# First block's second norm emitted earlier, its rows put into the query weights' tile, with closer weight slices

## The chip, the cores and the metric

The kernel runs on one core of one Trainium2 chip. The core has five engines that take their instructions from five queues, each in its own order: TensorE (PE: matrix products, with weight loads as a row of their own, PEld), VectorE (DVE), ScalarE (ACT), GpSimd (POOL) and SyncE (SP, which here only issues DMAs). An instruction waits at the head of its queue until the semaphores that it needs are set, and whatever stands behind it on that engine waits too. The metric is device microseconds of one execution: 1638.99 us is the median of three runs of the kernel before (1636.83 to 1641.09).

## The reference

One transformer block on 2048 rows of 512, with modulation by a vector c:

```python
mod = (_silu(c) @ w_mod).reshape(c.shape[0], 6, 1, -1)
sa, ca, ga, sb, cb, gb = (mod[:, 0], mod[:, 1], ..., mod[:, 5])
h = _layernorm(x, axis=-1) * (1 + ca) + sa
x = x + ga * _A_ref(h, A_wq, A_wk, A_wv, A_wo)      # 32 heads of 16, one k and one v for all heads
h = _layernorm(x, axis=-1) * (1 + cb) + sb
x = x + gb * _B_ref(h, B_w_gate, B_w_up, B_w_down)  # (h W_gate * h W_up) W_down, 1792 columns
```

The attention is an exact softmax: scores over 2048 keys, their maximum taken out, exponential, product with v, division by the sum, then the product with wo.

## The kernel before, in words

**Units and turns.** The 2048 rows are eight blocks (`sb`, 0 to 7) of 256 query rows. A block has four groups of 8 heads, so there are 32 units `u` (unit 5 is block 1, second group of heads). A unit runs through 16 key tiles of 128 keys, one per *turn*; `attend(u, kt)` writes out two turns. Time in the program is counted in *steps*, two per turn and 32 per unit, so step 176 is unit 5, turn 8. In every turn stand four score products for the exponentials (`sc`, L680 and L682, with their four ACT exponentials, L688), four score products that only serve the maximum of the next unit (`mx`, L610, each followed by a DVE maximum over 512 keys, L614), and eight float32 products of the exponentials with v (`pv`, L722), which need the exponentials of the turn before or of this turn's first half.

**Side work.** All other large products run as *side* groups (class `Group`, L519) in PSUM banks of their own: the q projection (`q_proj`, 16 groups), the wo product (`wo_work`), and per block 14 gate/up groups and two down groups of the FFN (`ffn_work`). Between the score products, which use 48 or 51 of the 128 rows of the PE array, stand *halves* of side products on 64 rows, so that two such products run beside each other. A turn is written in one of three styles: FEW has four side halves, MANY has eight, and NO_SIDE has none, because no side group may start. What may start is decided by `open_gate`: the FFN groups of block `sb` wait for `h2done`, that is for the block's second norm. Side work that has found no place by the last unit is done after it, in the *tail*, with whole products on 128 rows.

**The second norm of a block.** When a block's wo group ends, `wo_work`'s `fin` adds the residual on DVE (L808), takes statistics on DVE (`spread` L815, `aggr` L818) and then 1/sqrt on POOL: eight short instructions, `rv` to `nb` (L220 to L225, L821, L822). `nrm` then makes the normed rows `n2`; for block 0 that is one ACT instruction per 128 rows (L829), which reads what POOL has made. For block 0 (and 7) `ln2_work` transposes `n2` on PE in two *turns* of four transposes (L880), ACT puts scale and shift in (`hf`, L888), and POOL splits the result into a high and a low float16 half (L893, L894), into the tile `h2T`. Blocks 1 to 6 make their `h2` with DMA transposes. For block 0 `nrm` was put 7 and 12 ticks (a tick is half a turn) behind the end of the second wo group, and the two transposing turns were taken only when all q groups had ended (`all(q.ended() for q in qs)`), because `h2T` was a new tile on the place of the q weights `wq`.

**Weights.** `late_weights` loads 4 slices of wo, 32 of gate and up (128 x 448) and 14 of down. A slice is loaded by SP (L1022) into one of six places of the staging tile `kwb` and split on POOL two list items later in three instructions (L1164 or L1158, L1165, L1166). Items are spaced by `SPLIT_GAP` steps. The squares of the down rows for their norms are ACT instructions between them (L1076).

**q groups.** They read column block `ch` of `wq` (128 columns each). The last three are block 3's second to fourth, and two of these run behind the wo groups of block 0.

**PSUM.** Eight banks; `pv` and the running side group hold one each, and `sc` and `mx` products go round the rest in the order in which banks were used.

Of the kernel before, what the change touches and what calls it, by code (L numbers as in the profile page):

```python
# [34 lines left out]
SLOTS = (0, 1, 2, 3, 12, 13)  # L35
SUM_GAP = 4.0
SUM_LAG = 3
SPLIT_GAP = 2.5
LAST_GAP = 2.5
LATE_Q = 3  # L40
NORM_AT = (2, 9, 12, 16)
NBANK = 8
QPRE = 24
Q_LAG = 8
TR_WAIT = 11
TR_LAG = 4
H2_LAG = 2
NHF = 12
# [20 lines left out]
def adaln_mqa_glu_kernel(ctx: ExitStack, tc: tile.TileContext, x_in, wq_in, wk_in, wv_in, wo_in,  # L69
# [627 lines left out]
    def p_places(both):  # L697
        n = 9 * D
        for i in range(2):
            t = both[:, i * n:(i + 1) * n]  # L700
            p_sets.append((t[:, D:].bitcast(F32).rearrange("p (j t) -> p j t", j=4),
                           t[:, :8 * D].rearrange("p (j h t) -> p j h t", j=4, h=2)))
        for i, k in enumerate(kts16):
            nc.gpsimd.tensor_scalar(v16[:, 0, i], vst[:, k, :], 1.0, 0.0, op0=OP.mult, op1=OP.add)
            nc.gpsimd.tensor_tensor(v16[:, 1, i], vst[:, k, :], v16[:, 0, i], op=OP.subtract)

    def pv(v):
        u, kt = divmod(v, KT)
# [83 lines left out]
    def wo_work(sb):  # L792
        on_pool = 2 <= sb < NS - 2
        by_dma = 0 < sb < NS - 1

        def op(t):
            def f(i):
                ch, term = divmod(i, 3)
                ol, wl = TERMS[term]
                return [(och[sb, ch][:, ol, t * 128:(t + 1) * 128], wo[:, wl, ch, :])]  # L800
            return f

        def fin(t):
            row = 2 * sb + t

            def f(p):
                x1 = x1s[row]
                nc.vector.scalar_tensor_tensor(x1, p, sca[:, 7:8], x1, op0=OP.mult, op1=OP.add)  # L808
                s2 = work.tile([128, 1, 2], F32, name="st2", bufs=5)
                bs = work.tile([128, 6], F32, name="bs", bufs=4)  # L810
                nb = work.tile([128, 2], F32, name="nb", bufs=4)
                yt = {}

                def spread():
                    nc.vector.bn_stats(bs, x1)  # L815

                def aggr():
                    nc.vector.bn_aggr(s2[:, 0, :], bs)  # L818
                    yt["y"] = rstd_of(s2, 1)
                    if not on_pool:  # L820
                        nc.gpsimd.tensor_tensor(nb[:, 0:1], s2[:, 0, 0:1], yt["y"], op=OP.mult)  # L821
                        nc.gpsimd.tensor_scalar(nb[:, 1:2], nb[:, 0:1], -1.0, 0.0, op0=OP.mult, op1=OP.add)  # L822

                def nrm():
                    n2 = work.tile([128, D], F32, name="n2", tag="n2", bufs=2)
                    if on_pool:
                        nc.gpsimd.tensor_scalar(n2, x1, s2[:, 0, 0:1], yt["y"], op0=OP.subtract, op1=OP.mult)
                    else:
                        nc.scalar.activation(n2, x1, AF.Identity, bias=nb[:, 1:2], scale=yt["y"])  # L829
                    n2s[row] = n2  # L830
                    if not by_dma:
                        return
                    nc.gpsimd.tensor_tensor(n2, n2, cbb, op=OP.mult)
                    nc.gpsimd.tensor_tensor(n2, n2, sbb, op=OP.add)
                    n16 = work.tile([128, 2, D], F16, name="n16", tag="gf", bufs=4)
                    nc.gpsimd.tensor_scalar(n16[:, 0, :], n2, 1.0, 0.0, op0=OP.mult, op1=OP.add)
                    nc.gpsimd.tensor_tensor(n16[:, 1, :], n2, n16[:, 0, :], op=OP.subtract)
                    after(TR_LAG + (3 if sb < 2 else 0), lambda: ln2_turn(sb, t, n16))

                after(3, spread)  # L840
                after(4, aggr)
                n2f[row] = nrm
                if t == 1:
                    late = 3 if sb < 2 else 0
                    for j in range(2):
                        after((4, 9)[j] + late, n2f[2 * sb + j])
                    if sb == 0:
                        after(TR_WAIT + late, lambda: turns.extend(ln2_work(sb)))
            return f

        return [Group(3 * KC, op(t), fin(t), lambda t=t: load_x(2 * sb + t)) for t in range(2)]
# [12 lines left out]
    def ln2_work(sb):  # L864
        st = {}

        def tr(i):
            def f():
                if not h2s:
                    h2T = big.tile([128, 2, 2, KC, ST], F16, name="h2T", tag="wq")  # L870
                    both = big.tile([128, 2 * KC * S], F16, name="glu", tag="big")
                    n = 2 * FT * ST
                    glus.append(both[:, :n].rearrange("p (h f t) -> p h f t", h=2, f=FT))
                    p_places(both[:, n:])
                    h2s.update({s: h2T[:, s % 2] for s in range(NS)})
                st["p"] = ps_hold("mx")
                for k in range(2):
                    for t in range(2):
                        c = k * ST + t * 128
                        nc.tensor.transpose(st["p"][:, c:c + 128],  # L880
                                            n2s[2 * sb + t][:, (2 * i + k) * 128:(2 * i + k + 1) * 128], ident)
            return f

        def ev(i):
            def f():
                hf = work.tile([128, 2, ST], F32, name="hf", tag="g", bufs=2)
                for k in range(2):
                    nc.scalar.activation(hf[:, k, :], st["p"][:, k * ST:(k + 1) * ST], AF.Identity,  # L888
                                         bias=hsc[:, 2 * i + k, 0:1], scale=hsc[:, 2 * i + k, 1:2])
                ps_give(st["p"])  # L890
                eng = nc.vector if sb == NS - 1 else nc.gpsimd
                h = h2s[sb][:, :, 2 * i:2 * i + 2, :]
                eng.tensor_scalar(h[:, 0], hf, 1.0, 0.0, op0=OP.mult, op1=OP.add)  # L893
                eng.tensor_tensor(h[:, 1], hf, h[:, 0], op=OP.subtract)  # L894
# [14 lines left out]
    def ffn_work(sb):  # L909

        def glu():
            return glus[0]

        def op(f):
# [390 lines left out]
    def attend(u, kt):  # L1305
# [10 lines left out]
        def end_turn(kt):  # L1316
# [8 lines left out]
            v = pv_place(u * KT + kt - 1) if u + kt else None  # L1325
            if v is not None:
                pv(v)
            if not late_max() and turns and all(q.ended() for q in qs):
                _, f, post = turns.popleft()
                f()  # L1330
                posts.append(post)
# [36 lines left out]
    def hooks(u, i):  # L1368
        step = u * NSTEP + i
        if later_h and i % 2 and i > 4:  # L1370
            b1, k = later_h.popleft()
            h_halves(b1, (k,))
        side_step(step)
        since = i - out_at[0]
        if u > 0 and i >= 3 and since in NORM_AT:
# [95 lines left out]
```

## Time and profile before

| | |
|---|---|
| median of three runs | 1638.99 us (1636.83 to 1641.09) |
| the profiled execution's own time | 1637.85 us |
| its span, first to last instruction | 1635.6 us |
| mean granted TensorE clock | 0.997 |
| DVE maxima L614 | 2016 instructions, 1273.0 us busy |
| ACT exponentials L688 | 1824 + 224 instructions, 982.5 + 123.8 us busy |
| PE whole gate products L519 on 128 rows | 292 instructions, 64.0 us busy |
| PE half gate products L519 on 64 rows | 2104 instructions, 476.5 us busy |

Rows of a timeline read: start in us, duration in us, engine, line, operation, written tile <- read tiles, shape, how many merged, and in brackets the engine's idle time before it with what ended it. Rows that group instructions read: count, busy us, mean ns of one, and the idle time before them. PE rows overlap, since products are pipelined; the distance between starts is what a product costs.

### The profile page before, as it was taken

How to read it: one execution, taken by the hardware profiler on the slowest of the kernel's cores; microseconds unless marked ns; L12 is line 12 of the kernel's file. 1: busy time of each engine (PE TensorE's matmuls, PEld its weight loads, DVE VectorE, ACT ScalarE, POOL GpSimd, SP SyncE). 2: the span in 40 equal slices, each digit the busy share in tenths (PEclk: the TensorE clock that was granted, in tenths of full speed). 3: DMA queues.
4: the chain of work that ended last, by engine and by line, in shares of the span. 5: the costliest groups of instructions: out<-in, count | busy, mean ns of one | idle time of the engine just before them, and what ended most of it. 6: DMA issues, size and time to landing. Idle time of an engine off the chain costs nothing.

```text
span 1635.6 us, 41004 instructions
## 1 busy us (share of the span) xinstructions
PE 1617.4 (99%) x15853; PEld 746.9 (46%) x15853; DVE 1401.3 (86%) x2433; ACT 1220.8 (75%) x2421; POOL 955.7 (58%) x1316
## 2 busy tenths in 40 slices
PE   8999999999999999999999999999999999999999
PEld 4333333355533555335543455434545345444766
DVE  8999999899999999999999999999999999980211
ACT  6688878888777888778877788777878778878300
POOL 6857537875755566646656466653657556565422
PEclk9999999999999999999999999999999999999999
DMA  7213314243221001100011001100001001100100
GB/s 257 99 56 97 94 63 122 89 128 93 65 63 35 14 20 29 36 32 20 13 32 36 26 14 33 32 26 26 20 25 33 24 18 33 32 15 22 34 14 14
DMA packets 78994, 79.13 MB, mean 48 GB/s; under 512 B 30408, under 2 KB 59340, under 8 KB 78800
## 3 DMA queue, kind: packets, MB, share of 16 engines
q1 hardware_dynamic: 77744, 76.46, 14.9%
q8 instruction: 124, 2.03, 0.5%
q14 instruction: 70, 0.57, 0.1%
q10 hardware_dynamic: 1056, 0.07, 0.0%
HBM read 56.04 MB, written 17.05 MB: 45 GB/s over the span
## 4 chain that ended last, share of the span: by engine, by line
PE 93%; ACT 2%; POOL 2%; DVE 2%; issue 1%; DMA 0%; SPq 0%; ACTq 0%; POOLq 0%; DVEq 0%
PE side L519 42%; PE pv L722 29%; PE mx L610 8%; PE sc L682 8%; PE sc L680 3%; ACT P L688 1%; DVE mpart L614 1%; PE part L290 0%; DMA wmA<-in_w_mod_dram 0%; PE mxt L638 0%; PE pk L298 0%; PE sc L610 0%; POOL wg L1166 0%; POOL kwb L1164 0%; POOL q L556 0%
## 5 line engine op out<-in xcount | busy, mean ns | idle before, releaser
L614 DVE TENSOR_REDUCE mpart<-mx 128x1 f32<-128x512 f32 x2016 | 1273.0, 684 | 81.7 <-PE mx L610 73.9
L688 ACT ACTIVATE P<-sc 128x512 f32<-128x512 f32 x1824 | 982.5, 599 | 219.6 <-PE sc L682 177.4
L610 PE MATMUL mx<-kst,sst 48*128 48x512 f16 x2032 | 629.0, 377 | 2.1 <-ACT P L688 0.9
L682 PE MATMUL sc<-sst,kst 51*128 51x512 f16 x1792 | 597.7, 379 | 0.8 <-ACT P L688 0.3
L519 PE MATMUL side<-h2T,wg 64*128 64x256 f16 (+1 forms) x2396 | 540.5, 271 | 0.6 <-POOL h2T L893 0.3
L519 PE MATMUL side<-h2T,wu 64*128 64x256 f16 (+1 forms) x2396 | 538.2, 270 | 0.0
L722 PE MATMUL pv<-P,vst 128*32 128x512 f32 x3648 | 485.7, 605 | 0.7
L519 PEld LDWEIGHTS <-wg 64*128 64x128 f16 (+1 forms) x2396 | 226.0, 94 | 220.1 <-ACT P L688 160.4
L519 PE MATMUL side<-wd,glu 64*128 64x512 f16 (+1 forms) x1172 | 271.7, 377 | 0.4 <-ACT tok L685 0.2
L695 POOL TENSOR_TENSOR glu<-glu 128x512 f16<-128x512 f32 x224 | 259.4, 1158 | 18.7
L519 PEld LDWEIGHTS <-wu 64*128 64x128 f16 (+1 forms) x2396 | 226.4, 94 | 41.0 <-issue 3.9
L927 POOL TENSOR_SCALAR glu<-gf 128x256 f16<-128x256 f32 x112 | 45.9, 410 | 277.0 <-DVE gf L926 264.7
L610 PEld LDWEIGHTS <-sst 48*128 48x128 f16 x2064 | 190.2, 94 | 32.4 <-issue 17.0
L694 POOL TENSOR_SCALAR glu<-glu 128x512 f16<-128x512 f32 x224 | 138.3, 618 | 110.1 <-ACT glu L688 79.6
L682 PEld LDWEIGHTS <-kst 51*128 51x128 f16 x1792 | 162.9, 94 | 62.8 <-issue 50.3
L519 PEld LDWEIGHTS <-glu 64*128 64x128 f16 (+1 forms) x1172 | 98.7, 95 | 187.6 <-ACT P L688 69.1
L688 ACT ACTIVATE glu<-sc 128x512 f32<-128x512 f32 x224 | 123.8, 596 | 51.7 <-PE sc L682 50.1
L722 PEld LDWEIGHTS pv<-P,vst 128*32 128x32 f32 x3648 | 71.9, 108 | 143.6 <-issue 134.3
L926 DVE TENSOR_TENSOR gf<-side,g 128x256 f32<-128x256 f32 x112 | 46.7, 418 | 79.8 <-ACT g L924 69.8
L680 PE MATMUL sc<-sst,kst 51*128 51x256 f16 x512 | 96.9, 268 | 0.0
L519 PE MATMUL side<-h,wq 64*128 64x512 f16 (+1 forms) x372 | 95.0, 376 | 0.4 <-ACT P L688 0.4
L924 ACT ACTIVATE g<-side 128x256 f32<-128x256 f32 x112 | 42.3, 379 | 66.1 <-PE side L519 65.7
(248 smaller groups left out, 1131.4 us busy)
## 6 DMA issues: line engine op xcount, KB each, us to landing
pd<-ev SPq DMA_DIRECT2D x32, 256.0 KB
kwb<-in_B_w_gate_dram SPq DMA_DIRECT2D x32, 224.0 KB
kwb<-in_B_w_up_dram SPq DMA_DIRECT2D x32, 224.0 KB
sst<-qd SPq DMA_DIRECT2D x180, 32.0 KB
qd<-q SPq DMA_DIRECT2D x16, 256.0 KB
oc<-pd SPq DMA_DIRECT2D x64, 64.0 KB
rr<-ri SPq DMA_DIRECT2D x64, 64.0 KB
x<-in_A_x_dram SPq DMA_DIRECT2D x14, 256.0 KB
```

The source lines that it names most:

```text
L519: return nc.tensor.matmul(self.p[:, c * w:(c + 1) * w], left[rows], right[rows], start=start and c == 0, stop=stop and c == len(terms) - 1)
L610: nc.tensor.matmul(m, s[64 * a:64 * a + 48, t // 2, p, t % 2 * 128:(t % 2 + 1) * 128], w[64 * a:64 * a + 48, :], start=(i == 0), stop=(i = ...
L614: nc.vector.tensor_reduce(part, m, axis=AX.X, op=OP.max)
L680: nc.tensor.matmul(t[:, c * ST:(c + 1) * ST], keys, s[64 * a:64 * a + 51, c, p, :], start=True, stop=True)
L682: nc.tensor.matmul(t.rearrange("k (c n) -> k c n", c=2), keys, s[64 * a:64 * a + 51, :, p, :], start=True, stop=True)
L688: ex = nc.scalar.activation(ptl[u, kt, p, a], t, AF.Exp)
L694: nc.gpsimd.tensor_scalar(h[:, j, 0], t[:, j], 1.0, 0.0, op0=OP.mult, op1=OP.add)
L695: nc.gpsimd.tensor_tensor(h[:, j, 1], t[:, j], h[:, j, 0], op=OP.subtract)
L722: nc.tensor.matmul(pvb[u][32 * j:32 * j + 32, :], vt, ps[j], start=start and n == 0, stop=stop and n == len(terms) - 1)
L924: nc.scalar.activation(g, p[:, 0:ST], AF.Copy, scale=2.0 ** -45)
L926: nc.vector.tensor_tensor(gf, p[:, ST:2 * ST], g, op=OP.mult)
L927: nc.gpsimd.tensor_scalar(glu()[:, 0, f, :], gf, 1.0, 0.0, op0=OP.mult, op1=OP.add)
```

## The change

Eight edits:

- `nrm` of block 0 is put 6 ticks behind the end of each wo group, for each 128 rows apart (before: 7 and 12 behind the second), and `ln2_work`'s two turns 7 ticks behind the second (before 14).
- The turns no longer wait for the q groups.
- `h2` of all blocks lies in `wq` itself: even blocks in its columns 0 to 255, odd blocks in 256 to 511. The q groups that still run read columns 256 to 511.
- The tile for the FFN products (`glu`), which takes the place of the q groups' inputs, is taken at the first use.
- Block 0's two splits go from POOL to DVE.
- `SPLIT_GAP` is 2.2 steps instead of 2.5.
- The six short POOL instructions that split three tiles of v (L704, L705) go from the making of `h2T` to unit 9.
- `TR_WAIT` goes.

```diff
-SPLIT_GAP = 2.5
+SPLIT_GAP = 2.2
...
-        for i, k in enumerate(kts16):
-            nc.gpsimd.tensor_scalar(v16[:, 0, i], vst[:, k, :], 1.0, 0.0, op0=OP.mult, op1=OP.add)
-            nc.gpsimd.tensor_tensor(v16[:, 1, i], vst[:, k, :], v16[:, 0, i], op=OP.subtract)
+
+    def v_split(i):
+        k = kts16[i]
+        nc.gpsimd.tensor_scalar(v16[:, 0, i], vst[:, k, :], 1.0, 0.0, op0=OP.mult, op1=OP.add)
+        nc.gpsimd.tensor_tensor(v16[:, 1, i], vst[:, k, :], v16[:, 0, i], op=OP.subtract)
...
-                if t == 1:
+                if sb == 0:
+                    after(6, nrm)
+                    if t == 1:
+                        after(7, lambda: turns.extend(ln2_work(sb)))
+                elif t == 1:
                     late = 3 if sb < 2 else 0
                     for j in range(2):
                         after((4, 9)[j] + late, n2f[2 * sb + j])
-                    if sb == 0:
-                        after(TR_WAIT + late, lambda: turns.extend(ln2_work(sb)))
...
                 if not h2s:
-                    h2T = big.tile([128, 2, 2, KC, ST], F16, name="h2T", tag="wq")
-                    both = big.tile([128, 2 * KC * S], F16, name="glu", tag="big")
...
-                    h2s.update({s: h2T[:, s % 2] for s in range(NS)})
+                    h2s.update({s: wq[:, :, :, s % 2 * ST:(s % 2 + 1) * ST] for s in range(NS)})
...
-                eng = nc.vector if sb == NS - 1 else nc.gpsimd
+                eng = nc.vector if sb in (0, NS - 1) else nc.gpsimd
...
         def glu():
+            if not glus:
+                both = big.tile([128, 2 * KC * S], F16, name="glu", tag="big")
+                n = 2 * FT * ST
+                glus.append(both[:, :n].rearrange("p (h f t) -> p h f t", h=2, f=FT))
+                p_places(both[:, n:])
             return glus[0]
...
-            if not late_max() and turns and all(q.ended() for q in qs):
+            if not late_max() and turns:
...
+        if u == F16_FROM - 1 and i % 2 and i // 2 < len(kts16):
+            v_split(i // 2)
```

What that does to the order. In steps, block 0's first rows are normed at step 162 instead of 170 and its second at 168 instead of 174; the transposes stand behind the `pv` products of steps 170 and 172 instead of 176 and 178; the first FFN group's first product stands at step 180 instead of 184. Before, steps 176 to 182 (unit 5, turns 8 to 11) were written in the style without side halves, the first two of them with the transposes behind their `pv`; in the change only turns 8 and 9 are, and turns 10 and 11 have eight side halves each. Over the program 2120 gate products stand as halves instead of 2104, and 284 as whole ones in the tail instead of 292; the same for up. (Line numbers of the change differ by up to three.)

**POOL, from the end of the first rows' norm chain to the start of the second's** (`nb` ends a chain, `rv` starts one; `kwb`, `wu`, `wg` are a weight slice's three instructions). Before:

```order
L822 TENSOR_SCALAR nb<-nb 128x1
L1164 TENSOR_SCALAR kwb<-kwb,sca 128x448
L1165 TENSOR_SCALAR wu<-kwb 128x448
L1166 TENSOR_TENSOR wu<-kwb,wu 128x448
L1164 TENSOR_SCALAR kwb<-kwb,sca 128x448
L1165 TENSOR_SCALAR wu<-kwb 128x448
L1166 TENSOR_TENSOR wu<-kwb,wu 128x448
L220 TENSOR_SCALAR rv<-st_4543 128x1
```

In the change:

```order
L823 TENSOR_SCALAR nb<-nb 128x1
L1167 TENSOR_SCALAR kwb<-kwb,sca 128x448
L1168 TENSOR_SCALAR wu<-kwb 128x448
L1169 TENSOR_TENSOR wu<-kwb,wu 128x448
L1167 TENSOR_SCALAR kwb<-kwb,sca 128x448
L1168 TENSOR_SCALAR wu<-kwb 128x448
L1169 TENSOR_TENSOR wu<-kwb,wu 128x448
L1167 TENSOR_SCALAR kwb<-kwb,sca 128x448
L1168 TENSOR_SCALAR wg<-kwb 128x448
L1169 TENSOR_TENSOR wg<-kwb,wg 128x448
L219 TENSOR_SCALAR rv<-st_4549 128x1
```

Three slices instead of two stand between the chains; ahead of the first chain, from the q split with which POOL was last held up, there are two wo slices and six gate/up slices instead of two and five.

**ACT, from the end of unit 4 on** (`mt` is the maximum's row, `ev` the output of unit 4, `qf` a q group's, `n` the two norms, `hf` the transposed rows). Before:

```order
L643 ACTIVATE mt_4346<-mxt 16x128
L688 ACTIVATE P<-sc 128x512 x16
L733 ACTIVATE ev<-pv 128x512
L688 ACTIVATE P<-sc 128x512 x12
L554 ACTIVATE qf<-side,qvs 128x512
L829 ACTIVATE n_4713<-x_4224,nb,ry 128x512
L688 ACTIVATE P<-sc 128x512 x11
L829 ACTIVATE n_4825<-x_4371,nb,ry 128x512
L688 ACTIVATE P<-sc 128x512
L554 ACTIVATE qf<-side,qvs 128x512
L688 ACTIVATE P<-sc 128x512 x4
L888 ACTIVATE hf<-mx,hsc 128x256 x2
```

In the change:

```order
L642 ACTIVATE mt_4350<-mxt 16x128
L687 ACTIVATE P<-sc 128x512 x15
L830 ACTIVATE n_4528<-x_4228,nb,ry 128x512
L687 ACTIVATE P<-sc 128x512
L734 ACTIVATE ev<-pv 128x512
L687 ACTIVATE P<-sc 128x512 x11
L830 ACTIVATE n_4691<-x_4379,nb,ry 128x512
L687 ACTIVATE P<-sc 128x512
L553 ACTIVATE qf<-side,qvs 128x512
L687 ACTIVATE P<-sc 128x512 x4
L886 ACTIVATE hf<-mx,hsc 128x256 x2
L687 ACTIVATE P<-sc 128x512 x4
```

The first norm moves 13 exponentials ahead and the second 12; behind each stand the exponentials of the same turn and the next.

**DVE, from the second rows' statistics on** (`st` the statistics, `mpart` the maxima, `rc` a reciprocal of the softmax sums). Before:

```order
L818 BN_AGGR st_4543<-bs 128x2
L614 TENSOR_REDUCE mpart<-mx 128x1 x12
L750 RECIPROCAL rc<-rc 128x16
L614 TENSOR_REDUCE mpart<-mx 128x1 x29
L631 TENSOR_REDUCE mm<-mpart 128x16
```

In the change:

```order
L819 BN_AGGR st_4549<-bs 128x2
L613 TENSOR_REDUCE mpart<-mx 128x1 x11
L891 TENSOR_SCALAR wq<-hf 128x2x256
L892 TENSOR_TENSOR wq<-hf,wq 128x2x256
L613 TENSOR_REDUCE mpart<-mx 128x1
L751 RECIPROCAL rc<-rc 128x16
L613 TENSOR_REDUCE mpart<-mx 128x1 x3
L891 TENSOR_SCALAR wq<-hf 128x2x256
L892 TENSOR_TENSOR wq<-hf,wq 128x2x256
L613 TENSOR_REDUCE mpart<-mx 128x1 x26
```

Four instructions on 128 x 512 elements are new among the maxima, one pair ahead of each of two turns.

More of the change, by code (lines that the diff above doesn't have):

```diff
@@ L44 @@
 Q_LAG = 8
-TR_WAIT = 11
 TR_LAG = 4
@@ L869, in f @@
                 if not h2s:
-                    h2T = big.tile([128, 2, 2, KC, ST], F16, name="h2T", tag="wq")
-                    both = big.tile([128, 2 * KC * S], F16, name="glu", tag="big")
-                    n = 2 * FT * ST
-                    glus.append(both[:, :n].rearrange("p (h f t) -> p h f t", h=2, f=FT))
-                    p_places(both[:, n:])
-                    h2s.update({s: h2T[:, s % 2] for s in range(NS)})
+                    h2s.update({s: wq[:, :, :, s % 2 * ST:(s % 2 + 1) * ST] for s in range(NS)})
                 st["p"] = ps_hold("mx")
```

## Prediction

> **What bounds the kernel now.** I read the page's busy times and its chain first, then the timeline of the stretch that the change rewrites.
>
> ```profile
> span 1635.6 us, 41004 instructions
> PE 1617.4 (99%) x15853; PEld 746.9 (46%) x15853; DVE 1401.3 (86%) x2433; ACT 1220.8 (75%) x2421; POOL 955.7 (58%) x1316
> PE 93%; ACT 2%; POOL 2%; DVE 2%; issue 1%; DMA 0%; SPq 0%; ACTq 0%; POOLq 0%; DVEq 0%
> ```
>
> PE is busy 99% of the span and 93% of the chain that ended last. Nothing is gained by making another engine faster; time can only come from places where PE waits, or where its instructions are written in an order that leaves half of its rows unused. The change touches one such place, unit 5. A turn can be read there as the distance between the starts of the `pv` products. The first three rows are of an ordinary stretch in the style MANY, the others of turns 7 to 13 of unit 5:
>
> ```profile
> 469.60 1.07 PE L722 MATMUL pv<-P,vst 128*32 128x512 f32 x8
> 472.43 1.06 PE L722 MATMUL pv<-P,vst 128*32 128x512 f32 x8
> 475.27 1.06 PE L722 MATMUL pv<-P,vst 128*32 128x512 f32 x8
> ...
> 307.75 1.06 PE L722 MATMUL pv<-P,vst 128*32 128x512 f32 x8
> 310.22 1.06 PE L722 MATMUL pv<-P,vst 128*32 128x512 f32 x8
> 313.29 1.06 PE L722 MATMUL pv<-P,vst 128*32 128x512 f32 x8
> 317.23 1.07 PE L722 MATMUL pv<-P,vst 128*32 128x512 f32 x8
> 319.20 1.07 PE L722 MATMUL pv<-P,vst 128*32 128x512 f32 x8
> 322.91 1.06 PE L722 MATMUL pv<-P,vst 128*32 128x512 f32 x8
> 325.75 1.06 PE L722 MATMUL pv<-P,vst 128*32 128x512 f32 x8
> ```
>
> A turn with eight side halves takes 2.84 us (475.27 - 472.43). Turns 8 to 11 have none, and still the six turns from 307.75 to 325.75 take 18.00 us, 3.00 each: two sets of transposes stand in them, and PE waits. The windows view says how long (its columns: length, then busy us of PE, PEld, DVE, ACT, POOL):
>
> ```profile
> 307.75:325.75 18.00, 16.69 (x139) 6.25 (x138) 15.06 (x25) 15.35 (x31) 16.66 (x27) 1.00 0.36 112
> 462.00:473.00 11.00, 11.00 (x97) 3.52 (x93) 10.06 (x18) 8.60 (x17) 8.94 (x9) 1.00 0.17 51
> ```
>
> PE idles 1.31 us of 18.00 there and nothing in the ordinary stretch, so 1.3 us of waits, and the unused rows, are all that there is to win.
>
> **The change part by part.**
>
> *The tail.* One pair of turns gets sixteen side halves, which are eight whole products each of gate and up less behind the last unit:
>
> ```profile
> 1590.05 0.27 PE L519 MATMUL side<-h2T,wu 128*128 128x256 f16 x1
> ...
> 1590.26 0.27 PE L519 MATMUL side<-h2T,wu 128*128 128x256 f16 x1
> ```
>
> One gate and one up product take 0.21 to 0.22 us (1590.26 - 1590.05), so eight take **-1.7 us**. This part is sure, since the tail has no other engine in its way for that long.
>
> *Turns 8 to 11.* Two of them stay without side halves but lose the transposes; then DVE sets their length. Two become ordinary ones. The rows of DVE and of the transposes:
>
> ```profile
> 300.71 2.53 DVE L614 TENSOR_REDUCE mpart<-mx 128x1 f32<-128x512 f32 x4 [0.42 <-PE mx L610]
> 314.28 0.66 PE L880 MATMUL mx<-ident,n 128*128 128x128 f32 x4
> 322.36 0.27 PE L519 MATMUL side<-h2T,wg 64*128 64x256 f16 x1 [0.33 <-POOL h2T L893]
> ```
>
> Four maxima take 2.53 us. Six turns become 2 x 2.53 + 4 x 2.84 = 16.42 us instead of 18.00. The transposes go on costing 2 x 0.6 us on PE (the next product starts 0.6 behind their first), only in turns 5 and 6. Together 16.42 + 1.2 - 18.00 = **-0.4 us**. The wait of 0.33 us for POOL's split is in these 18.00 and goes.
>
> *The norms.* In the change ACT reaches each norm 12 or 13 exponentials sooner, and POOL reaches 1/sqrt one slice later. The rows of POOL, then of ACT:
>
> ```profile
> 287.07 0.24 POOL L220 TENSOR_SCALAR rv<-st 128x1 f32<-128x1 f32 x1 [0.41 <-DVE st L818]
> 289.58 0.64 POOL L1164 TENSOR_SCALAR kwb<-kwb,sca 128x448 f32<-128x448 f32 x1
> 291.97 0.65 POOL L1164 TENSOR_SCALAR kwb<-kwb,sca 128x448 f32<-128x448 f32 x1
> 295.90 0.23 POOL L220 TENSOR_SCALAR rv<-st 128x1 f32<-128x1 f32 x1 [1.51 <-DVE st L818]
> ```
>
> ```profile
> 288.70 2.19 ACT L688 ACTIVATE P<-sc 128x512 f32<-128x512 f32 x4 [0.69 <-PE sc L682]
> 290.78 0.59 ACT L733 ACTIVATE ev<-pv 128x512 f32<-128x512 f32 x1
> 297.60 2.15 ACT L688 ACTIVATE P<-sc 128x512 f32<-128x512 f32 x4 [0.75 <-PE sc L682]
> 299.64 0.68 ACT L554 ACTIVATE qf<-side,qvs 128x512 f32<-128x512 f32 x1
> 300.21 0.81 ACT L829 ACTIVATE n<-x,nb,ry 128x512 f32<-128x512 f32 x1
> 300.91 2.05 ACT L688 ACTIVATE P<-sc 128x512 f32<-128x512 f32 x4
> ```
>
> A slice takes POOL 2.39 us (291.97 - 289.58), a chain 2.51 (289.58 - 287.07). POOL was free at 287.07 - 0.41 = 286.66; with one slice more ahead the first chain runs from 289.05 to 291.56. ACT comes to the first norm behind the third of the four exponentials from 288.70, an issue every 0.52 us, thus at 290.26, and **waits 1.3 us**. The second chain stands three slices behind: 291.56 + 3 x 2.39 = 298.73, done at 301.24. ACT comes to it behind the third exponential from 297.60, at 299.1, or some 0.5 later if PE was held by the first: it waits 1.2 to 2.1 us, and I take 1.6. Behind each stand exponentials for which PE's `pv` and its PSUM banks wait. What a late ACT costs PE one row pair shows:
>
> ```profile
> 359.44 0.63 ACT L1076 ACTIVATE kwb<-kwb 128x512 f32<-128x512 f32 x1 [0.85 <-DMA kwb<-in_B_w_down_dram]
> ...
> 360.69 0.37 PE L610 MATMUL mx<-kst,sst 48*128 48x512 f16 x1 [0.56 <-ACT P L688]
> ```
>
> There ACT lost 0.85 + 0.63 = 1.48 us and PE 0.56, so about 0.9 was hidden; at 299.64 to 300.91 a q output and a norm took 1.27 us together and no wait of PE stands behind them. I let 1.1 us be hidden. The first norm is then late by 1.3 + 0.7 and costs 0.9, the second by 1.6 + 0.7 and costs 1.2: **+2.1 us**, between 0 (POOL gains a slice somewhere) and 2.5 (0.9 hidden).
>
> *The splits on DVE.* The trace has them for block 7, in the tail:
>
> ```profile
> L893 DVE TENSOR_SCALAR h2T<-hf x2: 426/523/620, 1552.1 to 1553.5; 128x512 f16<-128x512 f32 x2
> L894 DVE TENSOR_TENSOR h2T<-hf,h2T x2: 1035/1039/1043, 1552.6 to 1554.2; 128x512 f16<-128x512 f32 x2
> ```
>
> One pair takes 0.52 + 1.04 = 1.56 us and stands ahead of a turn's maxima, waiting for ACT's `hf`. A turn with transposes lasts 2.84 + 0.6, DVE needs 2.53 of it, so 0.91 is free: 0.65 per pair, **+1.3 us**. The bounds are 0 (the waits for ACT let DVE catch up) and 3.1 (nothing is hidden).
>
> *At nothing.* v's six splits of 128 x 32 go to unit 9; they are first used in unit 10, and POOL is not on the chain there. That block 0's splits leave POOL only shortens its queue. Slices come sooner on SP too: one load now stands ahead of six others.
>
> ```profile
> 262.51 2.71 SPq L575 DMA_DIRECT2D sst<-qd x6
> ```
>
> These are rows of q that the maxima's products read first some four turns later in the program, over 10 us, so the 0.45 us of one more issue ahead of them (2.71 / 6) is covered; without that cover it would cost 0.45 us once. The float16 tile in `wq` has the same row lengths for PE as `h2T` had. The row squares on ACT stand three steps apart in both orders; if one of their waits is added it costs 0.56 us as above.
>
> **Sum**: -1.7 - 0.4 + 2.1 + 1.3 = **+1.3 us** against the profiled execution's 1637.85, which lies 1.14 under the median of 1638.99. From the median: 1638.99 + 1.3 = **1640.3 us**.
>
> **The rivals.**
>
> *The new waits are hidden.* POOL's idle 0.41 and 1.51 us ahead of its chains, and ACT's 0.5 to 0.75 us of idle in each turn, speak for it; against it, that the norm's wait stands in ACT's own queue. Then only -1.7 - 0.4 = -2.1 is left: 1636.9 us.
>
> *DVE and POOL hold each other up.* In the change DVE splits in SBUF while POOL splits slices back to back. What this may cost two rows show, the same operation on 128 x 512:
>
> ```profile
> L272 DVE TENSOR_SCALAR xbig<-xbig,st,ry x6: 531/544/578, 11.1 to 30.6; 128x512 f32<-128x512 f32 x6
> L272 DVE TENSOR_SCALAR P<-P,st,ry x2: 877/896/915, 38.8 to 39.6; 128x512 f32<-128x512 f32 x2
> ```
>
> The second two ran beside POOL's splits of the first block's rows and took 0.35 us more. With 0.35 on each of four instructions the sum becomes +1.3 + 1.4 = +2.7, 1641.7 us. If each waits for a whole one of POOL's,
>
> ```profile
> 299.77 1.04 POOL L1166 TENSOR_TENSOR wu<-kwb,wu 128x448 f16<-128x448 f32 x1
> ```
>
> it is +1.3 + 4 x 1.04 = +5.5, 1644.5 us, slower by 0.33%. It becomes that much slower only when the mean wait is over (4.9 - 1.3) / 4 = 0.9 us per instruction; against it speaks that the two seen had 0.35. The Trainium skill, page "SBUF — State Buffer", section "Who interferes with whom", states such a rule: VectorE and GpSimd share one pair of SBUF ports, and a VectorE instruction in a two-port mode or with two SBUF inputs and a GpSimd instruction exclude each other for their whole length. The two rows of 0.88 and 0.92 us agree with it in kind; by it the higher of the two results above would come out.
>
> *The gate opens no sooner in time.* If the slices or `h2` come late, PE waits in turns 10 and 11 as long as it has won: +1.3 + 2.1 = +3.4, 1642.4 us. Against it: POOL's first eight gate/up slices stand ahead of the second norm's chain, near 298, and the first FFN product comes over 15 us behind.
>
> **How the numbers follow.** Less than 0.3% (4.9 us) is about what a measurement of this kernel can tell from no change. The forecast has 0.50; the hidden waits 0.25; DVE and POOL at 0.35 us 0.11, at a whole instruction 0.07; the late gate 0.03; and 0.04 is for more won than I can name, since the waits of PE in this stretch are 1.3 us and no row shows more. So faster 0.04, slower 0.07, within 0.89. The range goes from the hidden waits less the scatter of the runs (about 1.5), 1635.4, to the upper bounds of the norms and the splits, -2.1 + 2.5 + 3.1 = +3.5, with the same scatter: 1644.0.
>
> **What would show it.** Right: ACT's norm rows carry idle time released by POOL `nb`, 1.3 and 1.6 us; turns 1 to 6 of unit 5 grow by some 3.4 us beside the transposes, turns 8 to 13 take 16.4; the tail is 1.7 us shorter. Wrong: no idle time at these rows, or DVE's splits at well over 1.6 us a pair. The forecast falls if PE's idle time in unit 5 is not where ACT and DVE were late, or if units 6 to 31, which I leave as they are, differ by over 2 us.

## The result and the profile after

| | us |
|---|---|
| before, median of 6 runs | 1639.33 (1636.83 to 1641.09) |
| changed, median of 6 runs | 1651.25 (1647.90 to 1651.62) |
| ratio, 95% interval | 1.007 (1.006 to 1.008) |
| profiled execution, changed: time, span, mean granted clock | 1651.27, 1649.2, 0.994 |
| the same before | 1637.85, 1635.6, 0.997 |

The change makes the kernel 12 us slower, and 1640.3 us had been forecast with a range that ended at 1644.0. The page of the changed kernel (busy times, granted clock in 40 slices, shares of the chain that ended last):

```profile
span 1649.2 us, 41040 instructions
PE 1625.4 (99%) x15871; PEld 749.2 (45%) x15871; DVE 1402.7 (85%) x2437; ACT 1222.3 (74%) x2421; POOL 954.7 (58%) x1312
PEclk9899999999999999999999999999999999999999
PE 92%; POOL 3%; ACT 2%; DVE 2%; issue 1%; DMA 1%; SPq 0%; ACTq 0%; POOLq 0%; DVEq 0%
```

It looks like the page of before: PE 99%, nearly the same work. PE's busy time grew by 8 us (1625.4 - 1617.4) with 18 instructions more, so the same products took longer; that is the first hint at the granted clock, the share of full speed at which TensorE was let run. The place is found by the lengths of the units, each taken from the start of its first exponential to that of the next unit's first (in us, of the two profiled executions):

| | before | changed | difference |
|---|---|---|---|
| to the first exponential of unit 0 | 74.0 | 74.9 | +0.9 |
| unit 5 | 47.4 | 56.0 | +8.6 |
| unit 6 | 47.2 | 50.4 | +3.2 |
| unit 7 | 47.6 | 47.1 | -0.5 |
| units 8 to 30 | 1049.9 | 1053.1 | +3.2 |
| unit 31 and tail | 157.6 | 156.0 | -1.6 |
| span | 1635.6 | 1649.2 | +13.6 |

Units 0 to 4 agree to 0.1 us. (The first row is no effect of the change: a kernel below whose first 250 us are written as before had 75.1 us there; the granted clock falls once more, or not, in this stretch.) So 11.8 us lie in units 5 and 6. The timeline of unit 5 at the first norm and at the second (start, length, engine, and in brackets the idle time ahead and what ended it):

```profile
287.74 0.17 DVE L819 BATCH_NORM_AGGREGATE st<-bs 128x2 f32<-128x6 f32 x1
290.12 0.24 POOL L219 TENSOR_SCALAR rv<-st 128x1 f32<-128x1 f32 x1
292.70 0.81 ACT L830 ACTIVATE n<-x,nb,ry 128x512 f32<-128x512 f32 x1 [1.50 <-POOL nb L823]
294.06 0.39 PE L518 MATMUL side<-h,wq 64*128 64x512 f16 x1 [1.73 <-ACT P L687]
...
299.93 0.23 POOL L219 TENSOR_SCALAR rv<-st 128x1 f32<-128x1 f32 x1
302.51 0.81 ACT L830 ACTIVATE n<-x,nb,ry 128x512 f32<-128x512 f32 x1 [0.61 <-POOL nb L823]
303.86 0.39 PE L518 MATMUL side<-h,wq 64*128 64x512 f16 x1 [1.03 <-ACT P L687]
```

ACT waits for POOL's chain as forecast, 1.50 and 0.61 us, with an exponential behind it that PE needs; PE idles 1.73 and 1.03 us. Then the splits, on the same timeline:

```profile
308.44 0.93 DVE L891 TENSOR_SCALAR wq<-hf 128x512 f16<-128x512 f32 x1 [1.37 <-ACT hf L886]
309.40 1.01 DVE L892 TENSOR_TENSOR wq<-hf,wq 128x512 f16<-128x512 f32 x1
311.06 0.37 PE L681 MATMUL sc<-sst,kst 51*128 51x512 f16 x1 [1.73 <-DVE mpart L613]
...
314.11 0.52 DVE L891 TENSOR_SCALAR wq<-hf 128x512 f16<-128x512 f32 x1 [1.21 <-ACT hf L886]
314.67 0.69 DVE L892 TENSOR_TENSOR wq<-hf,wq 128x512 f16<-128x512 f32 x1
316.01 0.37 PE L681 MATMUL sc<-sst,kst 51*128 51x512 f16 x1 [1.02 <-DVE mpart L613]
```

A split waits in DVE's queue for ACT's `hf`, and the maxima stand behind it: DVE does no maximum for 1.37 + 0.93 + 1.01 = 3.3 us at the first pair and for 2.4 us at the second, and PE idles 1.73 and 1.02 us, until a maximum frees a score bank. The windows view shows what followed (length, then busy us and instructions of PE, PEld, DVE, ACT, POOL, the granted clock, DMA share, GB/s). The windows are 3.4 us long, since the record of the granted clock changes only at whole steps of 3.413 us:

```profile
310.40:313.80 3.40, 2.74 (x21) 0.98 (x21) 2.50 (x6) 1.34 (x3) 3.15 (x5) 1.00 0.27 70
313.80:317.20 3.40, 2.26 (x14) 0.44 (x11) 3.06 (x6) 2.46 (x6) 0.55 (x1) 1.00 0.00 0
317.20:320.60 3.40, 3.40 (x20) 0.82 (x16) 3.03 (x5) 2.52 (x5) 2.69 (x4) 0.51 0.00 0
320.60:324.00 3.40, 3.40 (x19) 0.64 (x15) 1.90 (x4) 1.68 (x3) 3.15 (x5) 0.50 0.56 170
324.00:327.40 3.40, 3.40 (x42) 1.70 (x34) 2.57 (x5) 2.36 (x6) 3.15 (x6) 0.99 0.45 133
```

For two windows PE has half its clock: 20 and 19 products where the next has 42 (which also holds more side halves). At most half of 6.8 us, 3.4 us, is lost while PE counts as busy; the first experiment below puts it at 2.6 us. In unit 6 the same happens for another reason:

```profile
356.07 0.63 ACT L1079 ACTIVATE kwb<-kwb 128x512 f32<-128x512 f32 x1 [2.31 <-DMA kwb<-in_B_w_down_dram]
...
357.33 0.37 PE L609 MATMUL mx<-kst,sst 48*128 48x512 f16 x1 [2.01 <-ACT P L687]
```

```profile
354.80:358.20 3.40, 1.39 (x17) 0.66 (x17) 1.97 (x4) 2.13 (x6) 3.15 (x6) 1.00 0.73 257
358.20:361.60 3.40, 3.40 (x25) 1.54 (x19) 0.93 (x2) 1.75 (x5) 2.00 (x3) 0.50 0.22 67
361.60:365.00 3.40, 3.40 (x44) 1.95 (x41) 2.91 (x6) 2.87 (x7) 0.00 (x0) 1.00 0.02 5
```

A row square on ACT waits 2.31 us for a slice's transfer in a stretch in which the DMA engines are 73% busy; PE idles 2.01 us and runs one window at half clock, 1.7 us more.

So PE's waits over 0.1 us in unit 5 sum to 5.6 us (1.73 + 1.03 + 1.73 + 0.12 + 1.02; 1.3 before) and the clock to 3.4 at most; that is up to 7.7 of its +8.6. In unit 6 it is 2.0 (0.6 before) and 1.7, which is 3.1 of +3.2.

### The profile page after: what moved, and what is told of

The parts are those of the page before. It is cut to its first block, busy times and chain, and to the rows that moved or that the text cites. A ratio compares the mean times of both kernels' runs of the same rounds, so it can differ in the third digit from the quotient of the medians.

```text
span 1649.2 us, 41040 instructions
## 1 busy us (share of the span) xinstructions
PE 1625.4 (99%) x15871; PEld 749.2 (45%) x15871; DVE 1402.7 (85%) x2437; ACT 1222.3 (74%) x2421; POOL 954.7 (58%) x1312
## 4 chain that ended last, share of the span: by engine, by line
PE 92%; POOL 3%; ACT 2%; DVE 2%; issue 1%; DMA 1%; SPq 0%; ACTq 0%; POOLq 0%; DVEq 0%
PE side L518 40%; PE pv L723 29%; PE sc L681 8%; PE mx L609 8%; PE sc L679 3%; ACT P L687 1%; DVE mpart L613 1%; PE misc L178 1%; PE pk L297 0%; PE part L289 0%; POOL kwb L1167 0%; PE mxt L637 0%; PE sc L277 0%; POOL wg L1169 0%; PE sc L609 0%
## 5 line engine op out<-in xcount | busy, mean ns | idle before, releaser
L518 PE MATMUL side<-wq,wg 64*128 64x256 f16 (+1 forms) x2404 | 543.3, 271 | 0.4 <-ACT tok L684 0.3
L518 PE MATMUL side<-wq,wu 64*128 64x256 f16 (+1 forms) x2404 | 541.0, 270 | 0.0
L929 DVE TENSOR_TENSOR gf<-side,g 128x256 f32<-128x256 f32 x112 | 46.5, 416 | 84.8 <-ACT g L927 65.8
```

What stands on the lines that cost most here:

```text
L518: return nc.tensor.matmul(self.p[:, c * w:(c + 1) * w], left[rows], right[rows], start=start and c == 0, stop=stop and c == len(terms) - 1)
L929: nc.vector.tensor_tensor(gf, p[:, ST:2 * ST], g, op=OP.mult)
```

## The experiments

Theory A: these waits, and the clock that falls after them, are the loss. Rivals: the clock falls for a reason of its own (B); a wait only moves to another engine (C); the norm costs wherever it stands (D); the row squares wait wherever they fall (E). The lengths of units are those of one profiled execution of each kernel, which with the slices 2.5 apart was 2.8 us faster than the median given.

| kernel | median us (runs) | ratio to before, 95% interval | unit 5 | unit 6 | unit 8 |
|---|---|---|---|---|---|
| changed | 1651.25 (6) | 1.007 (1.006 to 1.008) | 56.0 | 50.4 | 46.1 |
| splits on POOL | 1647.23 (5) | 1.0054 (1.0042 to 1.0066) | 50.9 | 50.9 | 46.1 |
| norms later | 1649.02 (6) | 1.0066 (1.0052 to 1.0080) | 53.6 | 49.9 | 46.1 |
| slices 2.5 apart | 1648.94 (5) | 1.0056 (1.0044 to 1.0068) | 52.1 | 46.2 | 49.9 |
| all three | 1646.23 (5) | 1.0040 (1.0028 to 1.0052) | 47.8 | 46.2 | 51.5 |
| row squares at lag 2 | 1647.52 (1) | | 55.9 | 46.3 | 45.9 |

### The splits back on POOL

```diff
-                eng = nc.vector if sb in (0, NS - 1) else nc.gpsimd
+                eng = nc.vector if sb == NS - 1 else nc.gpsimd
```

> The changed kernel with block 0's two splits back on POOL; all else as changed. Theory A (idle and the clock that follows it): in the changed kernel's trace PE idles 1.73 and 1.02 us behind the splits on VectorE, and from 317 to 324 us the granted clock is 0.5, which costs half of 6.8 us, 3.4 us. Both should go: 1651.3 - 2.75 - 3.4 = 1645.1 us, with the clock at 1.0 throughout unit 5, the norms' waits (1.73 and 1.03 us) still there, and 0.3 us of a new wait of the first gate and up products for POOL. Rival B (the clock falls there whatever PE does): only the waits go, 1648.5 us, clock 0.5 stays. Rival C (the splits' waits turn up again as waits for POOL): 1651 us.

Unit 5 fell by 5.1 us, about as theory A has it (2.75 + 3.4 less what comes new), and the clock stayed at 1.0 there, so rival B falls in this unit. PE's waits between 286 and 362 us (waiting engine and line, whom for, us in total, times, longest):

```profile
PE side L518 <- ACT P L687: 2.8, 2, 1.7
PE mx L609 <- ACT P L687: 2.5, 1, 2.5
PE mx L609 <- DMA sst<-qd: 0.6, 1, 0.6
```

The waits for DVE's maxima are gone, the norms' 2.8 us stand, and a new 0.6 us is for a load, not for POOL: rival C falls too. The time was 2 us above the expected 1645.1; the wait for the row squares, left in, grew from 2.0 to 2.5 us, and unit 25 took 48.2 us in place of 47.1. This run also gives the price of the half clock. The six turns from the `pv` products of turn 7 to those of turn 13 of unit 5, first here, then in the changed kernel:

```profile
312.14:329.14 17.00, 16.24 (x156) 7.07 (x155) 14.88 (x24) 13.45 (x26) 15.83 (x23) 1.00 0.43 134
316.31:335.30 18.99, 18.99 (x156) 7.46 (x155) 15.28 (x25) 13.21 (x25) 14.69 (x20) 0.82 0.40 120
```

The same 156 products took 17.00 us at full clock, 0.62 of it the wait for the load, and 18.99 us with the falls: 18.99 - 16.38 = 2.6 us for the half clock, less than the 3.4 expected.

### The norms a turn later

```diff
-                    after(6, nrm)
+                    after(8, nrm)
...
-                        after(7, lambda: turns.extend(ln2_work(sb)))
+                        after(9, lambda: turns.extend(ln2_work(sb)))
```

> The changed kernel with both norms of block 0 (and the transposes) two steps, one turn, later. Theory A: ScalarE no longer waits for POOL's chain of the inverse root, so PE's idle of 1.73 and 1.03 us in turns 1 and 4 goes; the splits' waits and the clock of 0.5 behind them stay: 1651.3 - 2.8 = 1648.5 us. Rival D (the norm itself, 0.81 us on ScalarE in a turn that has no room, makes the idle wherever it stands): 1651 us, with idle of about 1 us beside the norms at their new place.

The time came out as theory A had it, the parts did not quite: PE's idle time behind the norms went from 2.76 to 0.8 us, so some 0.4 us for each is the norm itself (part of D), the clock fell for one window in unit 5 instead of two, and the splits' waits, now in other turns, grew:

```profile
PE sc L681 <- DVE mpart L613: 3.6, 2, 2.2
PE mx L609 <- ACT P L687: 2.0, 1, 2.0
PE side L518 <- ACT P L687: 0.8, 2, 0.4
```

### The slices 2.5 steps apart again, and all three edits

```diff
-SPLIT_GAP = 2.2
+SPLIT_GAP = 2.5
```

> The changed kernel with the weight slices 2.5 steps apart again, as before the change. Theory A: in unit 6 ScalarE's row square waited 2.31 us for its slice's transfer, PE idled 2.01 us behind it and then ran 3.4 us at the granted clock 0.5. With the slices further apart the transfer is not the last of a burst, so the wait is at most the 0.85 us of before: 1651.3 - 2.0 - 1.7 = 1647.6 us, and no clock below 1.0 in unit 6. Rival E (the wait hangs on where the row squares fall among the q transfers, not on the gap): a wait of 2 us somewhere in unit 6 or 7 stays, 1651 us.

Unit 6 did what theory A said (50.4 to 46.2 us, no wait). Unit 5 fell too, by 3.9 us, which had not been expected: PE's idle time behind the norms went from 2.76 to 0.3 us, so it hung on how far POOL was behind with the slices, and the clock fell for one window there instead of two. But unit 8 grew by 3.8 us, which no theory had. PE's waits between 286 and 500 us:

```profile
PE sc L681 <- DVE mpart L613: 2.4, 2, 1.4
PE side L518 <- POOL wd L1169: 1.6, 3, 0.8
PE side L518 <- POOL wd L1168: 1.2, 1, 1.2
PE side L518 <- ACT P L687: 0.3, 1, 0.3
```

The FFN now starts sooner, so its down weights are wanted sooner; at the old distance POOL splits them 2.8 us too late. The closer slices are no free gift but what the earlier start needs.

> The changed kernel with all three of these edits. Theory A: 1651.3 - 2.75 - 3.4 - 2.8 - 3.7 = 1638.7 us, at or just below the kernel before (its median 1639.3), with granted clock 1.0 from 100 us to the end. Rival B (the clock falls whatever PE does): 1651.3 - 2.75 - 2.8 - 2.0 = 1643.8 us.

Unit 5 is at 47.8 us, 0.4 over the kernel before, and unit 6 at 46.2, 1.0 under it; so the three edits together take the stalls out of these two units, but for 0.8 us beside the norms. The 7.5 us missed against the expectation are above all unit 8's: 5.4 over the changed kernel, with a window of half clock at 471 us.

### The row squares

```diff
-ROW_LAG = 4
+ROW_LAG = 2
```

> The changed kernel with the row squares 2 items behind their loads in place of 4, and nothing else. Theory A (ScalarE's square waits for the slot that was loaded last): no wait of PE in unit 6 or 7 over 0.2 us, unit 6 at 46.2 us as in the two runs that had this edit among others, no fall of the clock there; unit 5 keeps its four waits of 1.0 to 1.7 us, and is 52.6 to 56 us long by whether the clock falls there. Rival E (the transfers' burst): unit 6 at 50 us.

Unit 6 came to 46.3 us, without a wait; the clock fell in unit 5 alone. The code says why the square was late: per item one row and one slice are loaded, six slots go round, so at a lag of 4 items a row's slot has been refilled by the row three items on, and ScalarE squares what was issued one item before. At a lag of 2 it is the row's own slot. By this reading of the code the lag of 4, in the kernel before too, squares another row than the one it stands for (the first three rows never), so a lag of 2 changes what is squared and not only when; the squares only serve a scale. The distance of the slices by itself was tried on the kernel before:

```diff
-SPLIT_GAP = 2.5
+SPLIT_GAP = 2.2
```

> The kernel before with the slices 2.2 steps apart, nothing else. If the closer slices alone make the row squares wait (theory G), PE idles 1 to 2.5 us in unit 6 or 7, where the kernel before idles 0.56 and 0.18 us, and the unit is up to 1.7 us longer by the clock. If it needs the change's earlier start of the slices' users too (theory H), unit 6 and 7 stay at 47.2 and 47.6 us or a little less.

Theory G, and more: 1647.61 us (one run, with one fall of the clock more near 124 us, in unit 1), units 5 and 6 at 52.0 and 50.3 us. PE's waits between 286 and 400 us:

```profile
PE side L519 <- POOL h2T L893: 3.2, 1, 3.2
PE mx L610 <- ACT P L688: 2.4, 1, 2.4
PE mx L610 <- ACT hf L888: 0.5, 1, 0.5
PE sc L682 <- ACT P L688: 0.3, 1, 0.3
```

The closer slices make the row square late, and they also crowd POOL so that block 0's splits come 3.2 us late: on this spacing splits on POOL at their old place cost more idle time than the 2.75 us of the splits on VectorE.

### The splits on VectorE alone

```diff
-                eng = nc.vector if sb == NS - 1 else nc.gpsimd
+                eng = nc.vector if sb in (0, NS - 1) else nc.gpsimd
```

> The kernel before with one part of the change alone: block 0's splits on VectorE. Theory A (a pair of splits, 1.2 to 1.9 us, stands between the maxima that free the score banks, and there is no room for it in a turn): idle of about 1 us or more behind each pair in turns 8 to 10 of unit 5, 2 to 3 us more in unit 5 than the 47.4 of before, and a clock fall (1.7 to 3.4 us) if both lie close. Rival F (it costs only in turns with eight side halves; turns 8 to 11 of before have none): unit 5 at 47.4 us or less.

One run, 1642.43 us, of which 1.5 us are a fall of the clock in unit 1 that the kernel before did not have; unit 5 at 50.2 us against 47.4, PE's waits for maxima 1.5 + 0.4 us there, and a clock fall:

```profile
316.80:320.20 3.40, 1.49 (x7) 0.39 (x7) 2.98 (x6) 2.97 (x6) 3.21 (x5) 1.00 0.28 83
320.20:323.60 3.40, 3.33 (x15) 0.60 (x15) 2.09 (x5) 0.85 (x2) 3.15 (x5) 0.50 0.84 251
```

So theory A, not F: the split on VectorE costs in turns without side halves as well.

### What idle time costs, measured by itself

```diff
+    STALLS = {(12, 8): 4, (14, 8): 6, (16, 8): 8, (18, 8): 10, (20, 8): 12, (22, 8): 14,
+              (24, 8): 6, (24, 12): 6, (26, 8): 8, (26, 12): 8, (28, 8): 6, (28, 10): 6}
+    idle_t = consts.tile([128, 128], F16, name="idle_t")
...
+        for _ in range(STALLS.get((u, i), 0)):
+            nc.scalar.activation(idle_t, cbb[:, 0:128], AF.Copy)
```

> The kernel before, with idle work on ScalarE: in units 12, 14, 16, 18, 20 and 22, at step 8, that is one place each, 4, 6, 8, 10, 12 and 14 extra operations of about 0.27 us; in units 24, 26 and 28 two places, two turns apart (6 and 6; 8 and 8) and one turn apart (6 and 6). Theory A (PE's idle time within a stretch of about 3.4 us lowers the clock): about 0.5, 1.0, 1.6, 2.1, 2.6 and 3.2 us of idle in PE; no fall of the clock up to 1.7 us, one of 3.4 us at 0.5 from 2.0 us on, which costs 1.7 us more; the pairs of two places may fall though each alone would not. Rival B (the clock falls for another reason, at units 5 and 6 whatever is done): no fall at any of the places.

| unit | PE's idle time at the place, us | half clock after it, us | unit longer than before, us |
|---|---|---|---|
| 12 | 0.91 | none | 1.0 |
| 14 | 1.63 | none | 1.7 |
| 16 | 2.27 | none | 2.3 |
| 18 | 2.97 | 6.8 | 6.0 |
| 20 | 3.64 | 3.4 | 5.3 |
| 22 | 4.36 | 6.8 | 7.3 |
| 24 | 1.59 and 1.30 | none | 3.2 |
| 26 | 2.19 and 2.09 | none | 4.5 |
| 28 | 1.59 and 1.53 | none | 3.2 |

Two things are shown. PE's idle time is paid in full (within 0.3 us where the clock stayed): none of it is made up later. And beyond some point the clock is halved for one or two windows, with nothing in the program at that place but idle time: rival B falls for good. One window cost 1.7 us (5.3 - 3.64), two cost 3.0 and 2.9 us. The point of 2.0 us that I had expected is not the right measure; what counts is how the idle time falls into the windows. The windows ahead of the falls of units 18 and 20 (903.20 and 1002.20), the two halved windows behind the former, and the windows of units 16 (811.00) and 26 (1288.90), behind which nothing fell:

```profile
811.00:814.40 3.40, 1.62 (x23) 1.43 (x25) 0.97 (x2) 2.82 (x8) 2.00 (x3) 1.00 0.07 22
903.20:906.60 3.40, 1.09 (x10) 0.16 (x8) 1.46 (x3) 3.12 (x11) 1.77 (x2) 1.00 0.34 114
906.60:913.40 6.80, 6.14 (x28) 1.54 (x30) 2.58 (x4) 2.96 (x7) 4.89 (x6) 0.50 0.00 0
1002.20:1005.60 3.40, 1.07 (x15) 0.95 (x17) 0.42 (x1) 2.76 (x9) 1.18 (x2) 1.00 0.00 0
1288.90:1292.30 3.40, 1.87 (x16) 0.35 (x12) 2.10 (x4) 3.18 (x10) 0.99 (x1) 1.00 0.16 44
```

The idle 2.27 us of unit 16 were cut by a boundary, so that its window still had PE busy for 1.62 us, and nothing fell; with 1.09 and 1.07 busy it fell. In unit 22 a whole window was idle.

### Toward a better version

The kernel called four here is the changed one with the splits on POOL, the norms later and the row squares at lag 2; five has in addition this, so that from block 2 on both groups of `wo` go ahead of all that waits; six is five with the slices 2.4 steps apart.

```diff
-            early = max(len(left) - LATE_Q, 0) if sb == 0 else int(len(left) > 2)
+            early = max(len(left) - LATE_Q, 0) if sb == 0 else int(len(left) > 2 and sb < 2)
```

| kernel | median us (runs) | ratio to before, 95% interval | unit 5 | unit 6 | units 21, 25 |
|---|---|---|---|---|---|
| four | 1643.57 (11) | 1.0023 (1.0014 to 1.0031) | 49.0 | 46.2 | 47.1, 48.1 |
| five | 1640.11 (11) | 1.0005 (0.9996 to 1.0014) | 48.9 | 46.2 | 46.4, 46.5 |
| six | 1638.62 (11) | 0.9995 (0.9986 to 1.0004) | 47.8 | 46.5 | 46.4, 46.5 |
| before, row squares at lag 2 | 1637.26 (11) | 0.9986 (0.9977 to 0.9995) | 47.4 | 46.2 | 46.2, 46.2 |

> The changed kernel with the splits of block 0 back on POOL, its norms one turn later, the slices 2.2 steps apart as changed (at 2.5 the down slices came too late in unit 8, 3.8 us), and the row squares 2 items behind their loads in place of 4, so that ScalarE squares a slice that landed long ago. Theory A: unit 5 at 47.8 us as in the run with three edits, unit 6 at 50.4 - 2.0 (idle) - 1.7 (clock) = 46.7 us, unit 8 at 46.1 us: 1639 us, no difference from the kernel before that can be told. Rival E (the wait of the row squares is for the burst of transfers, wherever they stand): unit 6 stays at 50 us, 1642.5 us.

Units 6 and 8 came as expected (46.2 and 46.1), rival E falls. Unit 5 kept 0.84 us of a wait for a load of scores' operands, and the median is 4.6 us over the expected 1639 (the runs go from 1640.4 to 1644.6); the granted clock of the profiled execution is 1.0 from 76 us to the tail. That execution was 1.9 us faster than the median; units 21 and 25 are 2.7 us longer in it than in the kernel before.

> As the run before it, and in blocks 2 and on the two groups of wo go ahead of all that waits, not behind one group of it. In the changed kernel SyncE is still issuing a transposing load (1.23 us) when the last half of unit 20's and 24's offsets is ready, PE waits 0.48 and 0.44 us for these offsets, and units 21 and 25 are 0.9 and 0.8 us longer than before. Theory: with wo sooner the transposing loads are issued a turn sooner, both units come back to 46.2 and 46.3 us, 1637.3 us in all. Rival: the units stay at 47.1 us (the wait has another cause), 1639 us.

Units 21 and 25 came down by 0.7 and 1.6 us. What held them in the changed kernel is seen in SyncE's timeline at the end of unit 21, first before, then changed, and in PE's wait in the latter. The offsets (`sst<-mt`) are the maxima of the next unit, unit 22, without which its scores cannot start:

```profile
1059.71 1.23 SPq L860 DMA_TRANSPOSE h2T<-n  x1
1062.14 1.22 SPq L648 DMA_DIRECT2D sst<-mt  x2
```

```profile
1077.41 1.23 SPq L863 DMA_TRANSPOSE wq<-n  x1
1078.74 1.22 SPq L647 DMA_DIRECT2D sst<-mt  x2
```

```profile
PE sc L681 <- DMA sst<-mt: 0.5, 1, 0.5
```

Before, 2.4 us lie between the transposing load and the offsets; in the changed kernel 1.3 us, of which the load's issue takes 1.23, and PE waits.

> As the run with the block's wo first, with the slices 2.4 steps apart, between 2.2 and 2.5. In the run at 2.2 PE waits 0.86 us in unit 5 for a load of the next unit's scores that stands behind the slices; at 2.5 unit 5 was 47.8 us, but the down slices came up to 2.8 us late in unit 8. Expected: unit 5 at 48 us, unit 6 at 46.2, unit 8 at 46 to 47; 1639.0 us, the same as before. Rival: the down slices are late here too (unit 8 at 48 to 50 us), 1642 us.

As expected: the wait for the load is gone and the down slices are in time (unit 8 at 46.1). This version of the change cannot be told from the kernel before, but it holds the lag of 2 as well, which the kernel before lacks.

> The kernel before with the row squares 2 items behind their loads. Theory: its waits of 0.56 and 0.18 us in units 6 and 7 go, and both units come nearer to the 46.2 and 46.8 us that the last runs had: 0.7 to 1.8 us less, 1638.0 us, at the bound of what can be told. Rival: the lengths of units 6 and 7 come from how the work falls into the turns, so only the 0.7 us go or nothing.

This one edit of the kernel before, which touches nothing else of the change, is the fastest measured: 0.14% (0.05 to 0.23%) less. Units 6 and 7 are 1.0 and 0.6 us shorter, more than the two waits of 0.56 and 0.18 us. Against this kernel the best version of the change, six, is 1.4 us slower by the medians (1638.62 - 1637.26).

## Why the prediction was wrong

*The tail* was right: -1.6 us against -1.7.

*Turns 8 to 11*, -0.4: right in the turns, short in the transposes. The 16.4 us for six turns came out where the clock stayed up (17.00 - 0.62 = 16.4 with the splits on POOL); in the changed kernel they took 18.99. But there the two turns that got the transposes took 3.77 us each in place of 2.84, so 0.9 us per set and not 0.6: 16.38 + 1.86 - 18.00 = +0.2 us. A small term.

*The norms*, +2.1: right in mechanism, measured +2.8 of idle (1.73 + 1.03). ACT's own waits, 1.50 and 0.61 us, sum to less than my 1.3 and 1.6, but of the 1.1 us that I let be hidden each time only 0.6 and 0.4 were: ACT was late by 1.50 + 0.81 and by 0.61 + 0.81 us.

*The splits on DVE*, +1.3: mis-sized by half. I priced the pair's own 1.56 us less a slack of 0.91, though I wrote that it waits for ACT's `hf`; that wait, 1.37 and 1.21 us at the head of DVE's queue, was left out of the sum. PE's idle time was 1.73 + 1.02 = 2.75. The 1.56 us were themselves read beside work of POOL (its rows of 0.91 us at 1552.14 and 0.84 us at 1553.03 in the trace of before). That the first pair took 1.94 us beside POOL's back-to-back slices, where POOL's own next two instructions took 0.81 and 0.88 in place of 0.64 and 0.57 us, and the second 1.21 while POOL did nothing from 314.35 us on, speaks for the rival of the two engines holding each other up (some 0.7 us); POOL's timeline there:

```profile
313.31 1.04 POOL L1169 TENSOR_TENSOR wu<-kwb,wu 128x448 f16<-128x448 f32 x1
317.74 0.62 POOL L554 TENSOR_SCALAR q<-qf 128x512 f16<-128x512 f32 x1 [3.39 <-ACT qf L553]
```

The Trainium skill, page "SBUF — State Buffer", section "Who interferes with whom", states such an exclusion; by the two pairs the trace agrees with it in kind.

*At nothing: the row squares and SP's order.* I priced an added row-square wait at 0.56 us, the size of the one seen before. It was 2.01, for the transfer issued last, and `ROW_LAG` alone removes it. SP's order I checked for q's loads in units 4 and 5 alone, and took these as covered; once the stalls were gone PE waited for them (0.6 to 0.9 us with the splits on POOL, in four and in five). The transposing loads of blocks 4 and 5 cost 1.7 us in units 21 and 25. Units 6 to 30, which I left as they are, differ by +5.9 us; over 2 us was to be the sign that the forecast falls.

*The clock* is the step that failed in kind. The sum added waits as if the granted clock stayed at 1.0. The page of before had it at 9 in all slices, and a stall of 1.67 us at 124 us stood in that trace without a fall; but the windows view of the same trace shows, before unit 0, that it can fall:

```profile
53.70:60.50 6.80, 6.80 (x34) 3.44 (x35) 6.80 (x19) 5.27 (x10) 6.55 (x8) 0.50 0.01 2
```

I took no account of the clock at all. The falls cost 2.6 + 1.7 = 4.3 us, more than any term of the sum.

Together, against the 13.6 us between the spans: +0.9 ahead of unit 0, -1.6 tail, +8.6 in unit 5, +3.2 in unit 6, -0.5 in unit 7, +1.7 in units 21 and 25. By the distances of the `pv` products of its turns, with the run with the splits on POOL between, the 8.6 us of unit 5 are +2.7 behind the norms, +3.1 behind the splits, +1.9 transposes, -1.6 in the six turns behind them (18.0 to 16.4) and +2.6 for the clock. The other +1.5 us of units 8 to 30 presumably came with the shift of all work by some half turns (five has 2.2 us there, with units 21 and 25 mended); which turns gain it was not traced, so its cause stays open. That v's splits in unit 9 cost nothing stands as argued: unit 9 took 46.7 us against 46.6; they were not tried apart.

## What to carry to other kernels

On a kernel whose PE is 99% busy, price an edit by the idle time that it puts into PE, and add up to half a clock window, 1.7 us, for each of one or two windows wherever that idle time comes to about half of a 3.4 us window; in turns with few or no side halves about a third was enough in three executions. A consumer that is put at the head of another engine's queue costs its wait for the producer plus its length, not its length. When a stage is started sooner, look up what else must come sooner with it (here the down weights, and a load's place in SyncE's queue); with all of that mended, and the lag of 2, the change came out even with the kernel before, and 1.4 us behind it where that has the lag of 2 too.

## What the runs showed of the hardware

The record of the granted clock changes at steps of 3.413 us alone, and shows it halved for 3.4 or 6.8 us at a time. In ordinary turns a window with PE busy for 1.39 us or less of 3.4 was always followed by half clock, one with 1.81 or more never; between them both occur: 1.63, 1.68 and 1.79 were (in the runs with the splits on POOL, with the norms later and with all three edits), 1.62 was not (unit 16 above), and 1.72 was in two of fourteen profiled executions at the same place near 124 us, here the kernel before with the splits on VectorE:

```profile
122.30:125.70 3.40, 1.72 (x24) 0.75 (x20) 1.22 (x4) 0.91 (x3) 3.24 (x4) 0.99 0.32 91
125.70:129.10 3.40, 3.40 (x16) 0.64 (x16) 2.12 (x4) 1.76 (x5) 3.05 (x4) 0.50 0.82 271
```

Where few or no side halves stand, 2.26 to 2.28 busy us were too few in three executions (the window from 313.8 us of the changed kernel, and its like with the slices 2.5 apart and with the row squares at lag 2), while with the norms later 2.25 us were enough. So the busy time alone does not settle it. That activity is counted by filled rows of the array might explain it, and was not tested.

The Trainium skill, page "TensorE: Matmul & The Clock Gate", section "Part 1: The HAM clock gate", states a free-running window of 3413 ns and two clocks; the trace agrees in the steps and in the shares of 1.0 and 0.5. The same section of the Trainium skill puts the lower clock after one idle window or more, about 3.4 us; here less was enough, 2.01 us of idle time at 357.33 in a window in which PE was busy for 1.39 us.
